# A two-block mixture-of-experts kernel: Sinkhorn's column sums as products with ones, and the first expert's gate applied one expert later

## The chip, the cores and the metric

The kernel runs on one core of a Trainium2 chip. The metric is the device time of one execution in microseconds (us); the median of three runs counts. A core has TensorE (PE in the profile, its weight loads PEld), VectorE (DVE), ScalarE (ACT), GpSimd (POOL) and SyncE (SP, which issues the DMAs). Each engine takes its own instructions strictly in program order, and waits on the others by semaphores.

## The reference, cut to what matters

The input passes through a thresholded attention, a first feed-forward block, and then the block that the change touches: eight experts, weighted by a gate that is balanced by eight Sinkhorn rounds.

```python
N, D = x.shape                      # 2304 tokens, 512 features
logits = x @ w_gate                 # E = 8 experts
P = np.exp(logits - logits.max())
for _ in range(8):
    P /= P.sum(1, keepdims=True) + 1e-09
    P /= P.sum(0, keepdims=True) + 1e-09
    P *= N / E
out = np.zeros((N, D), dtype=np.float32)
for e in range(E):
    h = np.maximum(x @ w1[e], 0.0)
    ye = h @ w2[e]
    out += P[:, e:e + 1] * ye
```

## The kernel before

After the attention, class `Moe` runs both feed-forward blocks as a list of units. Units 0 to 23 are the first block (kinds "a" and "b" in turn, three superblocks of 768 tokens); from unit 24 on there is one unit for each superblock, expert and quarter of the hidden features, in that order. Expert 0 of superblock 0 is units 24 to 27, expert 1 units 28 to 31, and so on. A unit's second products run during the next unit.

A unit has seven slots, and the order of all work is written out by hand in `run` (L775): in each slot `mm1` (L588) issues six first products into one of two PSUM banks, `px` or `py`; `pop` (L719) issues a share of the queued second products of the unit before (line L666, into `ye`; five in most slots, eight in slot 5); then one step of the generator `sinkhorn` (L748) is taken; then `evac` (L600) lets DVE and ACT read the bank: in slot 0 ACT copies `px` to `p1` (shown as `p`, L620), in slot 1 DVE makes `u` (L623), in slot 3 `v` (L626), in slots 4, 5 and 6 `c` (L640). In slots 2, 4, 5 and 6 ACT makes `hh`, the rounded Relu (L661), and one slot later DVE makes the rest `hl` (L662). Slots 0, 2 and 4 write `px`, the others `py`; slot 2 adds to what slot 0 left, slot 6 to what slot 5 left. So slot 4 may write `px` only when `hl` of slot 2 has read it, and slot 6 adds to `py` only when `c` of slot 5 has read it.

POOL prepares the next unit's weights in five pieces (`prep1`, L520): differences `wt` (L530, L533, L536) and the rests `w1l` (L537, L540, L542), with ACT's copies `w1h` between them. ACT's copy L539 waits for `wt` of L536, and L542 for that copy. DVE makes the rest `w2l` (L565) in slot 5.

The gate: `gate` (L733) computes the logits of a superblock; those of the last one are done in unit 25. `sinkhorn` starts there. It takes the maximum over all partitions (DVE L754, POOL `partition_all_reduce` L755), the exponential (ACT L758), and then eight rounds of two steps, one step a slot. The first step has the row sums, their reciprocals, the row scaling and the column sums on each partition (DVE, L761 to L765), and POOL's `partition_all_reduce` over the partitions (L766). The second step has four DVE operations (L768 to L771) that scale the columns. The rounds fill units 26, 27 and the first four slots of unit 28. `p`, the tile `prob` of 128 partitions x 18 chunks x 8 experts, is scaled in place.

`accumulate` (L708) takes the second products of a finished expert: expert 0 is copied to `acc` by ACT with the gate `p` as scale (L713), every later expert is multiplied by its gate and added by DVE (L715). For expert 0 of superblock 0 this falls in unit 28 and the first slots of unit 29.

Of the kernel before, what the change touches and what calls it, by code (L numbers as in the profile page):

```python
# [16 lines left out]
# the square of the float32 whose bits are a float64's high word at 2**-126  # L17
# [11 lines left out]
# when the x of the next superblock is split: (slots from the start of the last unit, slot that takes it)  # L29
SPLITS_AT = ((0, 0), (1, 1), (2, 2), (3, 3), (8, 4), (9, 5), (10, 6))  # L30
# pieces of conversion and products of W34 in each slot of two head pairs
# [20 lines left out]
def attention(k):  # L52
    """x^T (features on partitions) of all batches, with the W34 product as filler of the tensor engine."""
# [162 lines left out]
    def pv(j):  # L216
        """One product of a quarter's five: twenty a pair."""
# [102 lines left out]
class W34:  # L320
    """W34 = w3 @ w_out: float64 inputs to float32, then products, in pieces between the attention's."""
# [75 lines left out]
    def convert(self, s, more):  # L397
        """One more piece; it waits while the products still need the buffers."""
        self.slot = s
        self.owed += more  # L400
        if not self.owed or self.gen is None or self.held and self.nw3 - 3 >= self.mm // 12:
            return
        self.owed -= 1
        if next(self.gen, self) is self:
            self.gen = None
# [35 lines left out]
def to_f32(k, pool, raw, out):  # L441
    """Round float64 values, as pairs of 32-bit words, to float32; below float32's normal range gives zero."""
# [22 lines left out]
class Moe:  # L465
    """Both feed-forward blocks. First products by one level of Winograd's form of Strassen's algorithm:
    x (tokens x features) and the first weights are cut into 2 x 2 blocks, seven block products a unit."""

    # slot: (combination of x, combination of weights, bank, adds to the bank)
# [27 lines left out]
    def rest(self):  # L497
        """What the second products need, once there is room."""
# [21 lines left out]
    def prep1(self, u):  # L520
        """Pieces that make the seven combinations of a unit's first weights, in two exact parts."""
# [57 lines left out]
    def xsplit(self, s, slot):  # L579
        """The combination of x that the product of this slot takes, in two exact parts."""  # L580
# [19 lines left out]
    def evac(self, u, slot):  # L600
        """Combines the products; the later half of the work of the slot before comes first."""
# [106 lines left out]
    def accumulate(self, e, s, tc):  # L708
# [3 lines left out]
        if e == 0:  # L712
            nc.scalar.activation(acc, self.yb[tc], AF.Copy, scale=p)  # L713
        else:
            nc.vector.scalar_tensor_tensor(out=acc, in0=self.yb[tc], scalar=p, in1=acc, op0=ALU.mult, op1=ALU.add)  # L715
# [3 lines left out]
    def pop(self, slot):  # L719
        """One slot's share of the second products, more where the next slot's product waits for this one's."""  # L720
# [12 lines left out]
    def gate(self, s, slot):  # L733
        """A third of the logits of a superblock, in the bank that is free after this slot's product."""
# [13 lines left out]
    def sinkhorn(self):  # L748
        nc, p = self.nc, self.p
        small = self.pool.tile([128, 64], F32, name="small")  # L750
        m, g = small[:, 0:1], small[:, 1:2]
# [3 lines left out]
        nc.gpsimd.partition_all_reduce(g, m, 128, bass_isa.ReduceOp.max)  # L755
        yield
# [3 lines left out]
        for _ in range(8):  # L760
# [5 lines left out]
            nc.gpsimd.partition_all_reduce(gcol, col, 128, bass_isa.ReduceOp.add)  # L766
            yield
            nc.vector.tensor_scalar(out=gcol, in0=gcol, scalar1=1e-9, scalar2=None, op0=ALU.add)  # L768
            nc.vector.reciprocal(col, gcol)
            nc.vector.tensor_scalar(out=col, in0=col, scalar1=float(NTOK // E), scalar2=None, op0=ALU.mult)  # L770
            nc.vector.tensor_tensor(out=p, in0=p, in1=col.unsqueeze(1).to_broadcast([128, NCH, E]), op=ALU.mult)  # L771
# [126 lines left out]
```

## Time and profile before

| what | value |
|---|---|
| median of three runs | 2405.67 us (2404.77 to 2406.38) |
| span of the profiled execution | 2403.0 us |
| its own time | not recorded apart; the three runs lie 1.8 to 3.4 us above the span |
| PE busy | 2255.6 us, 94% of the span |
| DVE, ACT, POOL busy | 1344.7, 983.7, 1298.1 us |
| chain that ended last | PE 75%, DVE 13%, issue 8%, ACT 2%, POOL 1% |

The span runs from the first to the last instruction of the execution that the profiler took. Shares of the whole span mix stages: attention, first block and experts have different limits. The row of granted clock in the page's slices shows 9 (full) nearly everywhere; the lowest values, 7 and 6, stand in slices 15 and 16 of 40, where the Sinkhorn rounds run. An idle time in the profile stands with the instruction that ended it and the operation that released it; "issue" is time in which an engine waited for nothing that the profile shows. Instructions that switch the code of POOL (MODIFY_POOL_CONFIG, shown on its queue and as ISA in the order) take hundredths of a microsecond themselves.

### The profile page before, as it was taken

How to read it: one execution, taken by the hardware profiler on the slowest of the kernel's cores; microseconds unless marked ns; L12 is line 12 of the kernel's file. 1: busy time of each engine (PE TensorE's matmuls, PEld its weight loads, DVE VectorE, ACT ScalarE, POOL GpSimd, SP SyncE). 2: the span in 40 equal slices, each digit the busy share in tenths (PEclk: the TensorE clock that was granted, in tenths of full speed). 3: DMA queues.
4: the chain of work that ended last, by engine and by line, in shares of the span. 5: the costliest groups of instructions: out<-in, count | busy, mean ns of one | idle time of the engine just before them, and what ended most of it. 6: DMA issues, size and time to landing. Idle time of an engine off the chain costs nothing.

```text
span 2403.0 us, 30418 instructions
## 1 busy us (share of the span) xinstructions
PE 2255.6 (94%) x11408; PEld 1927.3 (80%) x11408; DVE 1344.7 (56%) x2385; ACT 983.7 (41%) x1709; POOL 1298.1 (54%) x1178
## 2 busy tenths in 40 slices
PE   5999999998989963999999999999999999999999
PEld 4566666587978853899999999999999899999998
DVE  8999999856464522444444463444444634444444
ACT  5777777633333410333333344333333443333332
POOL 5887777676666511544444554444445644444441
PEclk9999999999999976999999999999999999999999
DMA  5334344121111110122222122222221222222111
GB/s 155 95 104 121 112 119 120 56 87 53 53 53 69 47 35 18 53 70 71 71 71 71 59 91 71 70 71 71 71 68 56 96 71 71 71 71 71 58 66 53
DMA packets 52820, 177.63 MB, mean 74 GB/s; under 512 B 6592, under 2 KB 6592, under 8 KB 52672
## 3 DMA queue, kind: packets, MB, share of 16 engines
q1 hardware_dynamic: 52672, 175.68, 22.9%
q8 instruction: 90, 1.47, 0.3%
q14 instruction: 58, 0.48, 0.1%
HBM read 164.64 MB, written 11.01 MB: 73 GB/s over the span
## 4 chain that ended last, share of the span: by engine, by line
PE 75%; DVE 13%; issue 8%; ACT 2%; POOL 1%; SPq 0%; DMA 0%; POOLq 0%; ACTq 0%; DVEq 0%
PE ye L666 35%; PE py L596 19%; PE px L596 14%; PE pv L232 3%; DVE p L159 3%; DVE nmx L144 2%; PE s L139 1%; DVE qs L111 1%; PE t L195 1%; DVE c L651 1%; DVE cva L455 1%; DVE xl L585 1%; DVE cva L452 1%; PE w L423 1%; ACT e L153 1%
## 5 line engine op out<-in xcount | busy, mean ns | idle before, releaser
L542 POOL TENSOR_TENSOR w1l<-wt,w1h 128x1024 fp32r<-128x1024 f32 x120 | 290.8, 2423 | 324.2 <-ACT w1h L539 317.5
L666 PE MATMUL ye<-w2l,hh 128*128 128x512 f32 x1152 | 452.8, 393 | 3.3 <-DVE w2l L565 3.3
L666 PE MATMUL ye<-w2h,hl 128*128 128x512 f32 x1152 | 455.4, 395 | 0.0
L666 PE MATMUL ye<-w2h,hh 128*128 128x512 f32 x1152 | 453.7, 394 | 0.0
L661 ACT ACTIVATE hh<-c 128x384 fp32r<-128x384 f32 x288 | 151.4, 526 | 623.3 <-DVE c L640 623.3
L596 PE MATMUL py<-xh,w1h 128*128 128x384 f32 x960 | 326.7, 340 | 42.4 <-DVE c L640 32.8
L537 POOL TENSOR_TENSOR w1l<-raw,w1h 128x256 fp32r<-128x256 f32 x120 | 91.9, 766 | 493.7 <-ACT w1h L531 493.7
L596 PE MATMUL py<-xh,w1l 128*128 128x384 f32 x960 | 325.2, 339 | 0.3 <-POOL w1l L542 0.3
L596 PE MATMUL py<-xl,w1h 128*128 128x384 f32 x960 | 325.3, 339 | 0.0
L596 PE MATMUL px<-xh,w1h 128*128 128x384 f32 x720 | 244.5, 340 | 29.7 <-DVE hl L662 29.7
L666 PEld LDWEIGHTS ye<-w2l,hh 128*128 128x128 f32 x1152 | 217.6, 189 | 36.6 <-DVE w2l L565 3.7
L666 PEld LDWEIGHTS ye<-w2h,hl 128*128 128x128 f32 x1152 | 218.4, 190 | 32.8
L596 PE MATMUL px<-xh,w1l 128*128 128x384 f32 x720 | 244.0, 339 | 0.0
L596 PE MATMUL px<-xl,w1h 128*128 128x384 f32 x720 | 243.7, 338 | 0.0
L596 PEld LDWEIGHTS py<-xh,w1h 128*128 128x128 f32 x960 | 182.5, 190 | 68.9 <-DVE c L640 37.0
L666 PEld LDWEIGHTS ye<-w2h,hh 128*128 128x128 f32 x1152 | 218.1, 189 | 24.1
L596 PEld LDWEIGHTS py<-xl,w1h 128*128 128x128 f32 x960 | 182.6, 190 | 18.1
L623 DVE TENSOR_TENSOR u<-py,p 128x384 f32<-128x384 f32 x120 | 66.8, 557 | 214.6 <-PE py L596 212.4
L596 PEld LDWEIGHTS py<-xh,w1l 128*128 128x128 f32 x960 | 182.5, 190 | 0.6 <-POOL w1l L542 0.6
L530 POOL TENSOR_TENSOR wt<-raw 128x512 f32<-128x512 f32 x120 | 162.3, 1352 | 34.7 <-issue 21.0
L596 PEld LDWEIGHTS px<-xh,w1h 128*128 128x128 f32 x720 | 137.2, 191 | 45.3 <-DVE hl L662 31.3
L662 DVE SCALAR_TENSOR_TENSOR hl<-c,hh 128x384 fp32r<-128x384 f32 x288 | 166.2, 577 | 12.8 <-ACT hh L661 3.3
(127 smaller groups left out, 4448.5 us busy)
## 6 DMA issues: line engine op xcount, KB each, us to landing
raw<-in_e SPq DMA_DIRECT2D x192, 512.0 KB, 4.3
r<-in_qk SPq DMA_DIRECT2D x60, 288.0 KB, 6.6
wraw<-in_w SPq DMA_DIRECT2D x32, 512.0 KB, 4.5
raw<-w_a SPq DMA_DIRECT2D x12, 512.0 KB, 4.4
raw<-w_b SPq DMA_DIRECT2D x12, 512.0 KB, 3.2
raw<-w SPq DMA_DIRECT2D x12, 512.0 KB, 3.7
rv<-in_vv SPq DMA_DIRECT2D x16, 320.0 KB, 3.0
out<-acc SPq DMA_DIRECT2D x18, 256.0 KB, 2.0
```

The costliest lines, as they stand in the source:

```text
L111: nc.vector.scalar_tensor_tensor(out=dst, in0=rq[64:128, h, o:o + 288], scalar=0.125, in1=f32(dst), op0=ALU.mult, op1=ALU.subtract)
L144: nc.vector.tensor_reduce(out=nmx[:, s % 18:s % 18 + 1], in_=ps[:, :, 0:288], axis=AX.XY, op=ALU.max, negate=True)
L159: nc.vector.scalar_tensor_tensor(out=p, in0=ps[:, :, 0:288], scalar=thr[:, s % 18:s % 18 + 1], in1=e, op0=ALU.is_ge, op1=ALU.mult, accum_o ...
L232: nc.tensor.matmul(ps[0:64, 0:288], lhsT=l, rhs=r, start=i == 0, stop=i == 4)
L530: nc.gpsimd.tensor_tensor(out=t[:, 0:2], in0=raw[:, 1:3], in1=raw[:, 0:2], op=ALU.subtract)
L537: nc.gpsimd.tensor_tensor(out=wl[:, 0], in0=raw[:, 0], in1=f32(wh[:, 0]), op=ALU.subtract)
L542: nc.gpsimd.tensor_tensor(out=wl[:, 3:7], in0=t, in1=f32(wh[:, 3:7]), op=ALU.subtract)
L596: self.nc.tensor.matmul(out, lhsT=w[:, wi, o], rhs=x[xi][:, d], start=n == 0 and not adds, stop=n == 5, skip_group_check=True)
L623: tt(out=self.u2, in0=py, in1=self.p1, op=ALU.add)
L661: nc.scalar.activation(hi, src, AF.Relu)
L662: self.later.append(lambda: nc.vector.scalar_tensor_tensor(out=lo, in0=src, scalar=0.0, in1=f32(hi), op0=ALU.max, op1=ALU.subtract))
L666: self.queue.append((out.shape[-1], lambda: self.nc.tensor.matmul(out, lhsT=l, rhs=r, start=start, stop=stop, skip_group_check=True)))
```

## The change

Four things change. The column sums over the partitions are now one product of TensorE each: a tile `ones` (128 x 128, filled by POOL) as weights, the partial sums `col` as the 8 moving columns, into columns 384 to 391 of `px` or `py`, which the first products leave free. Adding 1e-9 reads PSUM, and the two multiplies that followed the reciprocal are one. The steps are placed anew: the maximum is issued at the end of unit 25, the exponential in slot 2 of unit 26, and the rounds begin in slot 3, with the product in the slot after the sums; products stand in slots 4 and 6 of unit 26, 1, 3 and 5 of unit 27, and 0, 2 and 4 of unit 28. And expert 0 of superblock 0 is copied without its gate; `acc` is multiplied by it when expert 1 is added, in unit 32. Besides, comments are gone, which moves line numbers.

```diff
@@ accumulate
-        if e == 0:
+        if e == 0 and s == 0:
+            nc.scalar.activation(acc, self.yb[tc], AF.Copy)
+        elif e == 0:
             nc.scalar.activation(acc, self.yb[tc], AF.Copy, scale=p)
         else:
+            if e == 1 and s == 0:
+                nc.vector.tensor_scalar(out=acc, in0=acc, scalar1=self.p[:, tc, 0:1], scalar2=None, op0=ALU.mult)
             nc.vector.scalar_tensor_tensor(out=acc, in0=self.yb[tc], scalar=p, in1=acc, op0=ALU.mult, op1=ALU.add)
@@ sinkhorn
+        ones = self.pool.tile([128, HT], F32, tag="c2", name="ones", bufs=2)[:, 0:128]
+        nc.gpsimd.memset(ones, 1.0)
...
         nc.gpsimd.partition_all_reduce(g, m, 128, bass_isa.ReduceOp.max)
+        yield
+        yield
         yield
...
             nc.vector.tensor_reduce(out=col, in_=p.rearrange("p c e -> p e c"), axis=AX.X, op=ALU.add)
-            nc.gpsimd.partition_all_reduce(gcol, col, 128, bass_isa.ReduceOp.add)
+            bank = yield
+            ps = bank[:, HT:HT + E]
+            nc.tensor.matmul(ps, lhsT=ones, rhs=col, start=True, stop=True, skip_group_check=True)
+            nc.vector.tensor_scalar(out=gcol, in0=ps, scalar1=1e-9, scalar2=None, op0=ALU.add)
+            nc.vector.reciprocal(col, gcol)
+            nc.vector.scalar_tensor_tensor(out=p, in0=p, scalar=float(NTOK // E),
+                                           in1=col.unsqueeze(1).to_broadcast([128, NCH, E]), op0=ALU.mult, op1=ALU.mult)
             yield
-            nc.vector.tensor_scalar(out=gcol, in0=gcol, scalar1=1e-9, scalar2=None, op0=ALU.add)
-            nc.vector.reciprocal(col, gcol)
-            nc.vector.tensor_scalar(out=col, in0=col, scalar1=float(NTOK // E), scalar2=None, op0=ALU.mult)
-            nc.vector.tensor_tensor(out=p, in0=p, in1=col.unsqueeze(1).to_broadcast([128, NCH, E]), op=ALU.mult)
-            yield
@@ run
-                next(sink, None)
+                if sink:
+                    try:
+                        sink.send(self.xy[1 if slot < 4 else 0])
+                    except StopIteration:
+                        sink = None
...
                         sink = self.sinkhorn()
+                        next(sink)
```

POOL from the start of Sinkhorn on, before (L755 and L766 are the reductions, an ISA row alone is a switch of POOL's code, L530 to L540 prepare the weights of units 27 and 28):

```order
L755 ISA
L755 ISA small<-small 128x1 [waits DVE_49]
L530 ISA
L530 TENSOR_TENSOR wt_7940<-raw_27_7772 128x512 [waits DMAHW0_49,Pool_49]
L533 TENSOR_TENSOR wt_7940<-raw_27_7772,wt_7940 128x256 [waits Pool_49]
L766 ISA
L766 ISA small<-small 128x8 [waits DVE_49]
L536 ISA
L536 TENSOR_TENSOR wt_7940<-raw_27_7772,wt_7940 128x256 [waits Pool_49]
L537 TENSOR_TENSOR w1l_7939<-raw_27_7772,w1h_7938 128x256 [waits PE_49,Activation_49]
L540 TENSOR_TENSOR w1l_7939<-raw_27_7772,w1h_7938 128x512 [waits Activation_49]
L766 ISA
```

The same place in the change, where L757 fills `ones` and L762 is the one reduction left:

```order
L757 MEMSET ones 128x128 [waits DVE_49]
L762 ISA
L762 ISA small<-small 128x1 [waits DVE_49]
L530 ISA
L530 TENSOR_TENSOR wt_7942<-raw_27_7772 128x512 [waits DMAHW0_49,Pool_49]
L533 TENSOR_TENSOR wt_7942<-raw_27_7772,wt_7942 128x256 [waits Pool_49]
L536 TENSOR_TENSOR wt_7942<-raw_27_7772,wt_7942 128x256 [waits Pool_49]
L537 TENSOR_TENSOR w1l_7941<-raw_27_7772,w1h_7940 128x256 [waits PE_49,Activation_49]
L540 TENSOR_TENSOR w1l_7941<-raw_27_7772,w1h_7940 128x512 [waits Activation_49]
L542 TENSOR_TENSOR w1l_7941<-wt_7942,w1h_7940 128x1024 [waits Activation_49]
L530 TENSOR_TENSOR wt_8087<-raw_28_7925 128x512 [waits DMAHW2_49,Pool_49]
```

The reductions between the weight pieces are gone, and with them all switches but one there and one back.

DVE in slots 3 and 4 of unit 27, before, from the row scaling on (`small` holds the sums and their reciprocals):

```order
L764 TENSOR_TENSOR prob<-prob,small 128x144 [waits DVE_49]
L765 TENSOR_REDUCE small<-prob 128x8 [waits DVE_49]
L662 SCALAR_TENSOR_TENSOR hl_8070<-px,hh_8069 128x384 [waits Activation_49]
L626 TENSOR_TENSOR v_3_8152<-py,u_27_1_8112 128x384 [waits PE_49]
L768 TENSOR_SCALAR small<-small 128x8 [waits Pool_49]
L769 RECIPROCAL small<-small 128x8 [waits DVE_49]
L770 TENSOR_SCALAR small<-small 128x8 [waits DVE_49]
L771 TENSOR_TENSOR prob<-prob,small 128x144 [waits DVE_49]
L640 TENSOR_TENSOR c_4_8172<-px,v_3_8152 128x384 [waits PE_49]
```

The same place in the change, from the row scaling of slot 2 to the first row of slot 4's block:

```order
L773 TENSOR_TENSOR prob<-prob,small 128x144 [waits DVE_49]
L774 TENSOR_REDUCE small<-prob 128x8 [waits DVE_49]
L778 TENSOR_SCALAR small<-py 128x8 [waits PE_49]
L779 RECIPROCAL small<-small 128x8 [waits DVE_49]
L780 SCALAR_TENSOR_TENSOR prob<-prob,small 128x144 [waits DVE_49]
L662 SCALAR_TENSOR_TENSOR hl_8064<-px,hh_8063 128x384 [waits Activation_49]
L626 TENSOR_TENSOR v_3_8144<-py,u_27_1_8105 128x384
L770 TENSOR_REDUCE small<-prob 128x18 [waits DVE_49]
```

The three operations behind the product (L778 to L780) now stand ahead of `hl` and `v` in slot 3; before, the sums stood there and the wait for POOL came in slot 4, ahead of `c`.

PE at the end of slot 3 of unit 27, before:

```order
L666 MATMUL ye_5146<-w2h_8000,hl_7919 128x512
L666 MATMUL ye_5147<-w2h_8000,hh_7918 128x512
L666 MATMUL ye_5147<-w2l_8044,hh_7918 128x512
L596 MATMUL px<-xh_4956,w1h_7938 128x384 [waits DVE_49]
L596 MATMUL px<-xl_4963,w1h_7938 128x384
L596 MATMUL px<-xh_4956,w1l_7939 128x384
```

And in the change:

```order
L666 MATMUL ye_5146<-w2h_7997,hh_7923 128x512
L666 MATMUL ye_5146<-w2l_8040,hh_7923 128x512
L666 MATMUL ye_5146<-w2h_7997,hl_7924 128x512
L666 MATMUL ye_5147<-w2h_7997,hh_7923 128x512
L666 MATMUL ye_5147<-w2l_8040,hh_7923 128x512
L777 MATMUL py<-small,ones 128x8 [waits DVE_49]
L596 MATMUL px<-xh_4956,w1h_7940 128x384 [waits DVE_49]
```

The product of `ones` and `small` stands behind the slot's five second products and ahead of the next slot's first product, which waits for DVE in both.

## Rows read from the trace of the kernel before

**Rows 1.** Windows: us, busy time of PE, PEld, DVE, ACT, POOL, then granted clock, DMA.

```profile
992.00:2380.00 1388.00, 1388.00 (x6965) 1252.49 (x6964) 636.63 (x1026) 487.49 (x828) 663.70 (x539) 1.00 0.21 70
845.69:991.41 145.72, 81.65 (x314) 70.52 (x312) 43.32 (x112) 24.35 (x43) 35.80 (x36) 0.73 0.08 25
```

**Rows 2.** Timelines of PE and ACT: start us, us, instruction, idle time before it.

```profile
845.69 0.34 PE L596 MATMUL px<-xh,w1h 128*128 128x384 f32 x1
...
846.73 0.39 PE L666 MATMUL ye<-w2h,hh 128*128 128x512 f32 x1
...
991.41 0.34 PE L596 MATMUL px<-xh,w1h 128*128 128x384 f32 x1
...
992.71 0.49 ACT L620 ACTIVATE p<-px 128x384 f32<-128x384 f32 x1 [0.90 <-PE px L596]
...
1008.25 0.49 ACT L620 ACTIVATE p<-px 128x384 f32<-128x384 f32 x1 [0.90 <-PE px L596]
```

**Rows 3.** Waits of the stretch 838 to 975 us: total, times, longest.

```profile
DVE small L768 <- POOL small L766: 79.6, 8, 12.6
...
PE px L596 <- DVE hl L662: 29.7, 3, 11.4
...
PE py L596 <- DVE c L640: 25.5, 3, 8.8
...
PE py L596 <- DVE u L623: 5.2, 1, 5.2
```

**Rows 4.** Timeline of POOL around the second reduction.

```profile
853.09 1.28 POOL L530 TENSOR_TENSOR wt<-raw 128x512 f32<-128x512 f32 x1 [7.18 <-issue]
854.45 0.72 POOL L533 TENSOR_TENSOR wt<-raw,wt 128x256 f32<-128x256 f32 x1
861.16 0.43 POOL L766 PARTITION_ALL_REDUCE small<-small  x1 [5.99 <-issue]
```

**Rows 5.** Timeline of PE: the end of its first idle time in unit 26.

```profile
863.10 0.69 PE L596 MATMUL px<-xh,w1h 128*128 128x384 f32 x1 [8.50 <-DVE hl L662]
```

**Rows 6.** Timeline of PE: the gate products of one slot.

```profile
842.99 1.85 PE L740 MATMUL px<-wg,x 128*128 128x8 f32 x16
```

**Rows 7.** Timeline of DVE: behind the second column sum, and the third row sum.

```profile
877.46 0.17 DVE L768 TENSOR_SCALAR small<-small 128x8 f32<-128x8 f32 x1 [11.48 <-POOL small L766]
...
878.33 0.55 DVE L640 TENSOR_TENSOR c<-py,v 128x384 f32<-128x384 f32 x1
878.80 0.55 DVE L662 SCALAR_TENSOR_TENSOR hl<-c,hh 128x384 fp32r<-128x384 f32 x1
...
880.40 0.30 DVE L761 TENSOR_REDUCE small<-prob 128x18 f32<-128x144 f32 x1
...
881.92 0.55 DVE L640 TENSOR_TENSOR c<-py,u 128x384 f32<-128x384 f32 x1
```

**Rows 8.** Timelines of POOL and DVE: subtractions that overlap, and one in unit 30.

```profile
970.39 2.38 POOL L542 TENSOR_TENSOR w1l<-wt,w1h 128x1024 fp32r<-128x1024 f32 x1
...
970.95 2.24 DVE L662 SCALAR_TENSOR_TENSOR hl<-c,hh 128x384 fp32r<-128x384 f32 x1 [3.31 <-ACT hh L661]
...
998.54 2.40 POOL L542 TENSOR_TENSOR w1l<-wt,w1h 128x1024 fp32r<-128x1024 f32 x1 [2.97 <-ACT w1h L539]
```

**Rows 9.** PE waits and windows with granted clock in two earlier stretches.

```profile
667.00 0.39 PE L666 MATMUL ye<-hl,w2h 128*128 128x256 f32 x1 [1.50 <-DVE hl L653]
...
803.61 0.45 PE L596 MATMUL py<-xh,w1h 128*128 128x384 f32 x1 [2.24 <-DVE c L640]
...
664.00:672.00 8.00, 5.50 (x35) 5.30 (x36) 5.26 (x9) 3.69 (x7) 4.84 (x5) 1.00 0.36 136
808.00:812.00 4.00, 2.98 (x12) 2.98 (x13) 2.55 (x4) 2.93 (x6) 1.28 (x2) 0.66 0.72 259
```

**Rows 10.** Groups by line and shape: two DVE operations of 512 elements.

```profile
L715 DVE SCALAR_TENSOR_TENSOR acc<-ye,prob,acc 128x512 f32<-128x512 f32 x126 | 91.9, 744 | 3.8 <-PE ye L666 3.8
...
L460 DVE TENSOR_SCALAR cvs<-cvq 128x512 int32<-128x512 int32 x40 | 17.6, 441 | 0.3
```

More of the change, by code (lines that the diff above doesn't have):

```diff
@@ L788, in run @@
             pass
-        sink = iter(())
+        sink = None
         gates = {8 * s + (12 if s + 1 < NSB else 9): s for s in range(NSB)}
@@ L809, in run @@
                 self.pop(slot)
-                next(sink, None)
+                if sink:
+                    try:
+                        sink.send(self.xy[1 if slot < 4 else 0])
+                    except StopIteration:
+                        sink = None
                 self.evac(u, slot)
```

## The prediction

> **What bounds the kernel now.** I read the windows first, then the waits of the stretch in which the Sinkhorn work runs, then the timelines of POOL, DVE and PE there. From 992 to 2380 us TensorE is busy 1388.00 of 1388.00 us at granted clock 1.00; in 845.69 to 991.41, four units of the first expert (units 26 to 29), it is busy 81.65 of 145.72 us at a mean clock of 0.73 [rows 1]. An edit there is worth what TensorE's idle and slow time in it is worth. How long should four units take? The same copy `p<-px` of slot 0 comes at 992.71 and at 1008.25, so an undisturbed unit is 15.54 us, one of its seven slots 2.2 us, and four units are 62.2 us. Unit 26 starts at 845.69, unit 30 at 991.41 [rows 2]. So the hole costs 145.72 - 62.16 = **83.5 us**, its clock loss included. The change can't win more here.
>
> Who ends the waits? DVE's first operation behind each reduction (L768) waits for POOL 8 times, 79.6 us in all; PE in turn waits 29.7 us for `hl`, 25.5 us for `c` and 5.2 us for `u`, all of them DVE operations that stand behind L768 in DVE's queue [rows 3]. On POOL a PARTITION_ALL_REDUCE takes 0.43 us, but it stands 5.99 us behind the operation before it, and the operation after a reduction stands 7.18 us behind that, with nothing waited for ("issue") [rows 4]: a round is 13.6 us of POOL, while its two slots of TensorE are 4.4 us.
>
> **What the change removes.** Eight reductions on POOL with those gaps (the order shows only TENSOR_TENSORs behind the first reduction), and DVE's wait for them. The first expert's ACT copies no longer need `p`. If nothing took their place, the gain would be 83.5 us.
>
> The Trainium skill speaks against the change: GPSIMD Engine Reference, section Engine selection, gives a reduction along partitions to GpSimd. Its section Instruction dispatch prices the first call of a freshly loaded kernel at about 6 us, which the 5.99 us of [rows 4] bears out; of a second gap behind the call it says nothing, and by that price alone the change would free 8 x 6 = 48 us of POOL's time (an estimate from that page), not 8 x 13.6 = 109.
>
> **What stays.** One reduction (the maximum, L755), whose result is now read in slot 2 of unit 26 instead of slot 0. The gap behind it still holds POOL until 853.09 [rows 4]. The weights of unit 27 then take 2 x 1.28 + 3 x 0.72 + 2.38 = 7.1 us [rows 4, 8] and end near 860.3; unit 27 starts at 845.69 + 15.54 = 861.2 and wants the last piece one slot later. So that gap is covered, with 3 us; without the cover unit 27 would wait. In the trace too TensorE ran through it: its first idle time in the stretch ends at 863.10 and is DVE's [rows 5]. Cost 0. The fill of `ones` stands ahead of that reduction in POOL's idle time: 0.
>
> **What is added on TensorE.** Eight products of 8 columns. Nearest row: 8 gate products (16 instructions) take 1.85 us [rows 6], 0.23 us each, so 1.85 us. Bounds: half of it if much lies beside other work, double if one product alone isn't pipelined, 0.9 to 3.7 us. I take 1.85.
>
> **What is added on DVE's way.** In a product slot DVE now waits for the product, does three small operations, and only then the slot's own work. Four such operations took from 877.46 to 878.33, 0.87 us; without the extra multiply 0.65. The column-sum block (five operations) takes from 880.40 to 881.92, 1.52 us [rows 7]. Six first products of a slot take 846.73 - 845.69 = 1.04 us, so five second ones take 1.15; ACT's copy comes 1.30 us after the slot's start, 0.26 us after the sixth [rows 2]. The new product's answer I put at 0.3 us after TensorE is through with its slot. From then on TensorE waits wherever the next slot's product needs what DVE does behind the block. The order tells where (slots 0 to 6):
> 1. Unit 26, slot 5 to 6: slot 6 adds to `py` after `c` of slot 5. DVE has from slot 4's product on 0.3 + 0.65 + 0.47 (`c`) + 1.52 + 0.55 (`c`) + 0.06 = 3.55 us to do; TensorE has slot 5, with eight second products 2.9 us: **0.7 us**.
> 2. Unit 27, slot 3 to 4: `px` is rewritten after `hl` has read it, and `hl` stands behind the three operations: 0.3 + 0.65 + 0.55 [rows 7] + 0.06 = **1.55 us**.
> 3. Unit 27, slot 5 to 6: the same with `c`: **1.55 us**.
> 4. Unit 28, slot 3 to 4: from slot 2's product on 0.3 + 0.65 + 1.52 + 0.55 + 0.06 = 3.1 us against slot 3's 2.2: **0.9 us**.
> The other four products (unit 26 slot 6, unit 27 slot 1, unit 28 slots 0 and 4) delay results that have a slot or more to spare: 0. Sum 4.7 us.
>
> **Collisions of DVE and POOL.** While POOL's `w1l` subtraction ran from 970.39 for 2.38 us, a DVE `hl` that began at 970.95 took 2.24 us instead of 0.55 [rows 7, 8]; it ended 0.4 us after POOL did. Both its inputs, `c` and `hh`, lie in SBUF. The row and the column scaling of `p` have two such inputs too; no row shows them beside POOL, which stood still then. Bounds: 0, or the 2.4 us of the POOL operation each time they meet. I take that they are held as `hl` was. Where do they meet? POOL is late in unit 26, so its last subtraction runs about 857.9 to 860.3; the block of slot 5 reaches its row scaling at about 858.9: held some 1.5 us, on stall 1. In unit 30 the subtraction starts 7.1 us into the unit (998.54) [rows 2, 8]; in unit 28 ACT has two `acc` copies ahead of the weight copy that it waits for, so about 8.4 us; the row scaling of slot 3 comes 6.6 + 0.25 + 0.3 + 0.65 + 0.84 = 8.6 us in: held up to 2.2 us, on stall 4. A few tenths decide whether they meet; I take 2. On stalls 2 and 3 a few tenths. Together **3.9 us**.
>
> The Trainium skill, GPSIMD Engine Reference, section Key points, says that GpSimd shares its SBUF interfaces with VectorE and contends with operations of two SBUF inputs. By it the 3.9 us belong in the sum; by the undisturbed scalings of p alone the sum would be 3.9 us smaller.
>
> **Clock.** After a wait of 2.24 us and others close behind it TensorE fell to the lower of its two levels (1.2 GHz): the mean of 808 to 812 is 0.66. After waits of up to 1.50 us it stayed at 1.00 (664 to 672) [rows 9]. Stalls 1 and 4, with the collisions 2.2 and 2.9 us, are as long as the first of these. I take one such spell, 4 x (1 - 0.66) = **1.4 us**; bounds 0 and four, 5.6 us.
>
> **The first expert's gate.** In unit 32 six DVE multiplies of 128x512: 0.44 us (nearest in kind: 512 elements, one tensor input) to 0.74 us (nearest in shape) [rows 10], 2.6 to 4.5 us in all, behind the slots' own DVE work. Their cover is DVE's idle half, 636.63 busy of 1388 us [rows 1]. Three fall together at the unit's end and put off `u` of the next unit by up to 1.5 us; slot 3 wants it, 4.4 - 1.04 - 0.26 - 0.55 = 2.5 us after it is normally done. Cost 0; at most 1 us, if they meet POOL too.
>
> **Sum.** 83.5 - 1.85 - 4.7 - 3.9 - 1.4 = 71.6 us. The span is 2403.0 us; the three times lie 1.8 to 3.4 us above it, and that part stays. 2403.0 - 71.6 = 2331.4, with the median's 2.67 us beside it **2334.0 us**.
>
> **The rivals.**
> A, the forecast: 2334, own range 2329 to 2339 (products 0.9 to 3.7, spells 0 to 2, collisions 1 to 5).
> B, no collision and no spell: 2405.67 - 83.5 + 1.85 + 4.7 = 2328.7. For it: undisturbed scalings within the 1.52 us block; against: `hl` of 2.24 us.
> C, collisions on all four stalls (another 1.5 us on each of 2 and 3) and a spell after each (3 x 1.4): 2334.0 + 7.2 = 2341. For it: a wait of 2.24 us began a spell; against: waits of 1.50 us did not.
> D, the gap behind a reduction isn't the reduction's, POOL keeps it, and only 8 x 5.99 us go: 2405.67 - 47.9 + 11.9 = 2370. Against it: behind another POOL operation the next starts at once (854.45 behind 853.09) [rows 4].
> The price on the Trainium skill's page, GPSIMD Engine Reference, Instruction dispatch, would make it D.
> E, **slower**: each round's product now stands in TensorE's own in-order queue; if the way from product over DVE's scalings and sums to the next product is longer than two slots, TensorE waits in every round. It decides from 71.6 / 8 = 9.0 us a round on. With 13.6 us, a wait as long as POOL's round, it is 2334 + 109 = 2443. Against: the way is 0.3 + 0.65 + 1.52 us plus DVE's own work, under 4.4, and the longest hold in the rows is 2.4.
> F, the change doesn't do what it says: TensorE's idle time came from something that stays, about 2405. Against: 60.4 us of it end on DVE operations queued behind L768 [rows 3].
>
> **How the numbers follow.** A 0.66, B 0.13, C 0.14, D 0.03, E 0.02, F 0.02. The likeliest is A, 2334.0. The range 2326 to 2342 holds A, nearly all of B and more than half of C, some 0.85. Faster by over 0.2% (4.8 us, about what a measurement of this kernel can tell from no change) are A to D, 0.96; within it F, 0.02; slower E, 0.02.
>
> **What would show it.** In the changed profile: one PARTITION_ALL_REDUCE, and no "issue" gaps on POOL after 853; unit 26 to unit 30 in about 74 us; waits of PE at exactly those four places, ended by `c`, `hl`, `c` and `hl`, the first and the last 2 to 3 us; a scaling of `p` of over 1 us beside a `w1l`; one or two spells of low clock; no change from unit 30 on. Wrong would be: PE waiting for the new product's own input, a wait for `w1l` in unit 27, or for `u` in unit 33.

## The result, and the profile after

The changed kernel takes **2337.83 us** (median; 2337.07 to 2341.5) where the kernel before takes 2405.22 (2403.77 to 2406.38): ratio 0.9722, 95% interval 0.9708 to 0.9736, 67.4 us less. The forecast was 2334.0, with 2326 to 2342 as its range.

Where did the time go? Cut both spans where unit 26 and unit 30 start. Windows (us, busy time of PE, PEld, DVE, ACT, POOL, granted clock, DMA), of the kernel before:

```profile
0.00:845.69 845.69, 766.29 (x4040) 587.43 (x4041) 654.51 (x1232) 468.47 (x833) 598.57 (x604) 0.98 0.30 89
991.41:2403.00 1411.59, 1407.66 (x7057) 1269.30 (x7055) 646.87 (x1042) 490.91 (x834) 663.70 (x539) 1.00 0.21 70
```

and of the changed kernel, the three parts and a piece of the last:

```profile
0.00:849.02 849.02, 769.41 (x4040) 591.05 (x4041) 653.99 (x1232) 468.56 (x833) 598.63 (x605) 0.98 0.30 89
849.02:925.12 76.10, 67.21 (x329) 59.48 (x328) 46.21 (x105) 23.92 (x43) 31.81 (x28) 0.98 0.14 48
925.12:2336.70 1411.58, 1407.63 (x7057) 1269.30 (x7055) 651.43 (x1048) 490.88 (x834) 664.05 (x539) 1.00 0.20 70
...
925.00:2315.00 1390.00, 1390.00 (x6976) 1254.36 (x6975) 641.78 (x1033) 488.51 (x831) 664.05 (x539) 1.00 0.20 70
```

The last part is the same to 0.01 us (1411.59, 1411.58), and from 925 to 2315 TensorE is busy all the time, the gate's six multiplies in unit 32 included. Four units of the first expert take **76.10 us** instead of the 145.72 of [rows 1]: 69.6 less, to a floor of 62.2. The first part, which the change hardly touches (the maximum and the fill of `ones` stand at its end), took 3.3 us longer in this execution. 69.6 - 3.3 = 66.3 is the difference of the spans (2403.0, 2336.7); the profiled execution's own time was 2338.47.

TensorE's waits of the stretch, from its timeline (start us, us, instruction, idle time before it):

```profile
866.02 0.44 PE L596 MATMUL py<-xh,w1h 128*128 128x384 f32 x1 [3.05 <-DVE c L640]
868.73 0.41 PE L596 MATMUL px<-xh,w1h 128*128 128x384 f32 x1 [0.35 <-DVE small L778]
...
873.64 0.39 PE L777 MATMUL py<-small,ones 128*128 128x8 f32 x2 [0.28 <-DVE small L774]
879.93 0.44 PE L596 MATMUL px<-xh,w1h 128*128 128x384 f32 x1 [1.30 <-DVE hl L662]
886.48 0.44 PE L596 MATMUL py<-xh,w1h 128*128 128x384 f32 x1 [1.31 <-DVE c L640]
891.31 0.45 PE L596 MATMUL py<-xh,w1h 128*128 128x384 f32 x1 [0.30 <-DVE small L778]
896.34 0.45 PE L596 MATMUL py<-xh,w1h 128*128 128x384 f32 x1 [0.26 <-DVE small L778]
900.84 0.45 PE L596 MATMUL px<-xh,w1h 128*128 128x384 f32 x1 [2.04 <-DVE hl L662]
```

Four long ones, at the four places of the forecast, each ended by the operation forecast there: 3.05, 1.30, 1.31 and 2.04 us, in place of waits such as the 8.50 us of [rows 5]. Four short ones of 0.26 to 0.35 us were not forecast: three wait for DVE's addition (L778) to read the product with ones out of the bank whose other columns the next first product writes, and one is the product with ones waiting for its own input, the partial sums (L774).

POOL's timeline, the reduction that is left and three operations behind it:

```profile
848.86 0.57 POOL L762 PARTITION_ALL_REDUCE small<-small  x1 [9.67 <-DVE small L761]
856.25 1.28 POOL L530 TENSOR_TENSOR wt<-raw 128x512 f32<-128x512 f32 x1 [6.83 <-issue]
...
861.09 2.46 POOL L542 TENSOR_TENSOR w1l<-wt,w1h 128x1024 fp32r<-128x1024 f32 x1
...
897.33 2.38 POOL L542 TENSOR_TENSOR w1l<-wt,w1h 128x1024 fp32r<-128x1024 f32 x1 [3.94 <-ACT w1h L539]
```

One PARTITION_ALL_REDUCE, 6.83 us of "issue" behind it (7.18 in [rows 4]), and no such gap later.

DVE's timeline, the column scaling (L780), the adding of 1e-9 (L771) and the row scaling (L773), beside POOL's weight work and undisturbed, with the row sum (L770) and the reciprocal (L772) between them:

```profile
860.49 0.81 DVE L780 SCALAR_TENSOR_TENSOR prob<-prob,small 128x144 f32<-128x144 f32 x1
...
861.69 0.28 DVE L770 TENSOR_REDUCE small<-prob 128x18 f32<-128x144 f32 x1
862.01 1.57 DVE L771 TENSOR_SCALAR small<-small 128x18 f32<-128x18 f32 x1
863.62 0.27 DVE L772 RECIPROCAL small<-small 128x18 f32<-128x18 f32 x1
863.92 1.13 DVE L773 TENSOR_TENSOR prob<-prob,small 128x144 f32<-128x144 f32 x1
...
874.51 0.31 DVE L780 SCALAR_TENSOR_TENSOR prob<-prob,small 128x144 f32<-128x144 f32 x1
...
875.53 0.18 DVE L771 TENSOR_SCALAR small<-small 128x18 f32<-128x18 f32 x1
...
876.04 0.31 DVE L773 TENSOR_TENSOR prob<-prob,small 128x144 f32<-128x144 f32 x1
...
897.75 2.14 DVE L773 TENSOR_TENSOR prob<-prob,small 128x144 f32<-128x144 f32 x1
```

Either scaling takes 0.31 us alone. Begun 0.42 us into a subtraction of 2.38 us the row scaling takes 2.14, much as `hl` did in [rows 8] (2.24). And L771, which has one tensor input, takes 1.57 instead of 0.18. Ahead of TensorE's first long wait the excess is (0.81 - 0.31) + (1.57 - 0.18) + (1.13 - 0.31) = 2.71 us, ahead of the fourth 2.14 - 0.31 = 1.83.

### The profile page after: what moved, and what is told of

Its sections match the earlier page's. It is cut to its first block, busy times and chain, and to the rows that moved or that the text cites. A ratio compares the mean times of both kernels' runs of the same rounds, so it can differ in the third digit from the quotient of the medians.

```text
span 2336.7 us, 30411 instructions
## 1 busy us (share of the span) xinstructions
PE 2244.3 (96%) x11424; PEld 1919.8 (82%) x11424; DVE 1351.6 (58%) x2383; ACT 983.4 (42%) x1709; POOL 1294.5 (55%) x1171
## 3 DMA queue, kind: packets, MB, share of 16 engines
q8 instruction: 90, 1.47, 0.3%
## 4 chain that ended last, share of the span: by engine, by line
PE 79%; DVE 14%; issue 3%; ACT 2%; DMA 0%; SPq 0%; ACTq 0%; DVEq 0%
PE ye L666 37%; PE py L596 20%; PE px L596 15%; DVE p L159 3%; PE pv L232 3%; DVE nmx L144 2%; DVE qs L111 1%; PE s L139 1%; DVE c L651 1%; PE t L195 1%; DVE cva L455 1%; PE w L423 1%; DVE cva L452 1%; DVE xl L585 1%; ACT e L153 1%
## 5 line engine op out<-in xcount | busy, mean ns | idle before, releaser
L530 POOL TENSOR_TENSOR wt<-raw 128x512 f32<-128x512 f32 x120 | 162.3, 1353 | 20.7 <-issue 6.8
L661 ACT ACTIVATE hh<-px 128x384 fp32r<-128x384 f32 x96 | 47.4, 494 | 276.2 <-PE px L596 276.2
```

Of the source, the lines that this page charges most:

```text
L530: nc.gpsimd.tensor_tensor(out=t[:, 0:2], in0=raw[:, 1:3], in1=raw[:, 0:2], op=ALU.subtract)
L661: nc.scalar.activation(hi, src, AF.Relu)
```

## The experiments

The theory: the gain is the reductions' gaps off POOL; what is left between 76.1 and 62.2 us is waits at the four places, lengthened by DVE and POOL meeting, and a spell of low clock. Rivals: the gap is not the reduction's own (D), the late gate has a part in it, or the rest belongs to the rounds wherever they stand.

| run | time, beside before on the same chip (us) | ratio (95%) | four units (us) |
|---|---|---|---|
| the change | 2337.83, 2405.22 | 0.9722 (0.9708 to 0.9736) | 76.10 |
| e1 no rounds | 2325.22, 2407.41 | 0.9661 (0.9647 to 0.9675) | 63.49 |
| e2 a copy for each round's reduction | 2338.21, 2407.41 | 0.9714 (0.9699 to 0.9728) | 76.33 |
| e3 late gate alone | 2407.29, 2407.41 | 0.9999 (0.9990 to 1.0009) | 146.42 |
| e4 no weight work | 2330.55, 2407.41 | 0.9683 (0.9669 to 0.9697) | 69.34 |
| e5 evacuation first in slots 3, 5 | 2333.65, 2406.27 | 0.9690 (0.9672 to 0.9707) | 72.97 |
| e6 evacuation first in all slots | 2334.34, 2406.27 | 0.9695 (0.9677 to 0.9713) | 74.21 |
| e7 rounds spread | 2329.18, 2406.38 | 0.9684 (0.9670 to 0.9697) | 68.74 |
| e8 the same, w2h first | 2330.35, 2406.38 | 0.9687 (0.9674 to 0.9700) | 67.73 |
| e9 the change again | 2337.11, 2406.38 | 0.9714 (0.9701 to 0.9728) | 77.16 |
| e10 steps merged | 2333.34, 2407.72 | 0.9694 (0.9681 to 0.9707) | 68.17 |

The times are medians; the last column is read from one profiled execution each (that of e5 took 2340.63 us).

**e2: is the gap the reduction's own?** In the kernel before, POOL copies each column sum instead of reducing it, so the sum over the partitions is left out; every wait between DVE and POOL stays.

```diff
-            nc.gpsimd.partition_all_reduce(gcol, col, 128, bass_isa.ReduceOp.add)
+            nc.gpsimd.tensor_scalar(out=gcol, in0=col, scalar1=1.0, scalar2=None, op0=ALU.mult)
```

> The kernel before, with each round's POOL reduction replaced by a POOL copy of the partial sums (left out: the sum over partitions). Theory, the gaps around the reduction are its own and are what TensorE paid for: POOL's issue gaps go, units 26 to 29 take 66 to 76 us, time 2326 to 2338 us. Rival D of the prediction, the gap behind a reduction isn't the reduction's: about 2370 us. Second rival, the hop DVE to POOL to DVE is the cost whatever POOL does: over 2390 us.

76.33 us for the four units and 0.9714: the change's own numbers, without its products or its gate. That they agree so closely is chance: e2 has other waits of TensorE (3.70, 0.89, 1.16 and 2.64 us) and a mean clock of 0.93 instead of 0.98. POOL's timeline:

```profile
854.95 0.73 POOL L533 TENSOR_TENSOR wt<-raw,wt 128x256 f32<-128x256 f32 x1
855.66 0.28 POOL L766 TENSOR_SCALAR small<-small 128x8 f32<-128x8 f32 x1
855.92 0.72 POOL L536 TENSOR_TENSOR wt<-raw,wt 128x256 f32<-128x256 f32 x1
...
861.26 0.23 POOL L766 TENSOR_SCALAR small<-small 128x8 f32<-128x8 f32 x1 [2.71 <-DVE small L765]
861.46 2.37 POOL L542 TENSOR_TENSOR w1l<-wt,w1h 128x1024 fp32r<-128x1024 f32 x1
```

The copy stands between weight operations with no gap on either side. So both gaps of [rows 4] go with the reduction, and D falls. That each round still goes to POOL and back makes DVE wait 4.5 us in all, in three places (79.6 us in [rows 3]).

But the gaps don't come with every reduction. Once in the kernel before, two of them stand one behind the other, with no weight operation between (POOL's timeline):

```profile
939.41 0.43 POOL L766 PARTITION_ALL_REDUCE small<-small  x1 [5.75 <-issue]
944.07 0.40 POOL L766 PARTITION_ALL_REDUCE small<-small  x1 [4.23 <-DVE small L765]
951.57 1.25 POOL L530 TENSOR_TENSOR wt<-raw 128x512 f32<-128x512 f32 x1 [7.10 <-issue]
```

The second begins 0.1 us after DVE's sum is there (943.97), and DVE waits 0.53 us for it. So POOL stands still where it changes from weight operations to a reduction or back, seven times each way in the eight rounds, and not because of the reduction alone. Whether it would have been enough to keep the weight operations out from between the reductions was not tried.

**e3: the late gate alone**, on the kernel before.

```diff
-        if e == 0:
+        if e == 0 and s == 0:
+            nc.scalar.activation(acc, self.yb[tc], AF.Copy)
+        elif e == 0:
...
+            if e == 1 and s == 0:
+                nc.vector.tensor_scalar(out=acc, in0=acc, scalar1=self.p[:, tc, 0:1], scalar2=None, op0=ALU.mult)
```

> The kernel before with the second part of the change alone: expert 0 copied unscaled, its gate applied with expert 1. Theory, it is a matter of freedom for the placing and gives little by itself, since DVE and POOL hold TensorE up anyway: 2402 to 2406 us. Rival, ACT's wait of 13.2 us for the gate held up TensorE (the wait of 3.3 us for w2l at 975 and the low clock behind it): 2395 to 2400 us. The six multiplies: no wait of TensorE in units 32 and 33; if they cost, up to 1 us more.

No difference: 0.9999, within a tenth of a per cent either way, and PE's first wait is 8.50 us as in [rows 5]. The wait for `w2l` that the rival meant stays too (3.54 us, 3.33 before). In the kernel before a copy on ACT did wait for the last scaling of `p` (its timeline):

```profile
961.23 0.69 ACT L713 ACTIVATE acc<-ye,prob 128x512 f32<-128x512 f32 x1 [13.21 <-DVE prob L771]
```

In e3 none does, and nothing comes of it: DVE and TensorE are late anyhow. In the profile after, the copies begin at 895.23, 9.5 us ahead of the last scaling (904.78), so there the late gate lets the rounds end later. What it is worth in that place was not tried.

**e1: no rounds at all**, the floor of this program.

```diff
-        for _ in range(8):
+        for _ in range(0):
```

> The changed kernel without its eight Sinkhorn rounds (left out: both normalisations; the maximum and the exponential stay). Theory, the hole of 83.5 us is the rounds' alone and the one reduction left is covered: units 26 to 29 take 62 to 63 us, the time is 2405 - 83.5 = about 2322 us (2320 to 2325). Rival, part of the hole or of the 15.6 us between 2337.8 and 2322 belongs to something that stays (the first reduction, the late gate, the front of the program): 2326 or more, with TensorE waits left in units 26 to 29.

63.49 us, 1.33 above the floor of 62.16 and a little over the expected 62 to 63. One wait is left, in unit 27 (PE's timeline, and ACT's in the unit before):

```profile
867.53 0.50 PE L666 MATMUL ye<-w2l,hh 128*128 128x512 f32 x1 [1.02 <-DVE w2l L565]
...
860.53 1.06 ACT L539 ACTIVATE w1h<-wt 128x1024 fp32r<-128x1024 f32 x1 [4.90 <-POOL wt L536]
861.49 1.04 ACT L560 ACTIVATE w2h<-raw 128x1024 fp32r<-128x1024 f32 x1
```

The gap behind the one reduction makes `wt` late, so ACT's copy `w1h` (L539) waits 4.90 us; `w2h` and `hh` stand behind it. DVE's `hl` then comes late and runs beside POOL's last subtraction (2.26 us instead of 0.55), and `w2l` behind it takes 2.32 instead of 1.22. I had looked for `w1l` alone and said "covered": it costs 1.0 us where no other wait hides it. The wait of 1.02 us costs 1.33, some 0.3 more than the idle time that the profile gives it.

**e4: without POOL's and ACT's weight work.** Units 27 to 29 take the first weights of unit 26; the preparation of theirs is left out. Everything else is the changed kernel.

```diff
+        if u in (27, 28, 29):
+            self.w1[u] = self.w1[26]
+            return
```

> The changed kernel with units 27 to 29 taking unit 26's first weights (left out: POOL's and ACT's preparation of three units' weights, so POOL stands still beside the rounds). Theory, DVE's operations on p were held by POOL's subtractions: L771 and L773 take 0.18 and 0.31 us in all rounds, the wait for c in unit 26 falls from 3.05 to about 0.6 us, the wait for hl in unit 28 from 2.04 to about 0.8, no low clock behind it; time 2337.8 less 3.5 to 5.5, 2332 to 2334.5 us. Rival, the waits come from the place in DVE's queue alone: they stay, 2336 to 2339 us.

69.34 us against 76.10, at granted clock 1.00. The window:

```profile
849.78:919.12 69.34, 65.35 (x330) 58.19 (x328) 38.77 (x105) 18.41 (x34) 10.38 (x10) 1.00 0.16 54
```

The block that held up stall 1 (DVE's timeline; lines are 3 higher here):

```profile
862.27 0.18 DVE L774 TENSOR_SCALAR small<-small 128x18 f32<-128x18 f32 x1
862.48 0.27 DVE L775 RECIPROCAL small<-small 128x18 f32<-128x18 f32 x1
862.78 0.31 DVE L776 TENSOR_TENSOR prob<-prob,small 128x144 f32<-128x144 f32 x1
```

0.18 and 0.31 us again. Stalls 2 and 3 stay at 1.31, stalls 1 and 4 shrink to 0.34 and 0.24: by 3.05 - 0.34 = 2.71 and 2.04 - 0.24 = 1.80 us, to a few hundredths the excess that DVE's rows gave (2.71 and 1.83). They shrink further than expected (0.6 and 0.8), and the time, 2330.55, lies below the expected 2332 to 2334.5. So collisions (4.5 us) and the spell (1.7, below) make up 6.2 of the 6.8 us between the two kernels.

**e5 and e6: the evacuation ahead of the Sinkhorn step**, in slots 3 and 5 or in all: the operation that TensorE needs no longer stands behind the step.

```diff
+                ahead_of = slot in (3, 5)    # e6: True
+                if ahead_of:
+                    self.evac(u, slot)
...
-                self.evac(u, slot)
+                if not ahead_of:
+                    self.evac(u, slot)
```

> The changed kernel with DVE's own work of the slot ahead of the Sinkhorn step in slots 3 and 5 (hl and v, c and hl first). Theory, the four long TensorE waits come from the place of the Sinkhorn step in DVE's queue: all four go (3.05, 1.30, 1.31, 2.04 us and what the restarts add, some 8.3 us, and the spell of low clock, 1.7 us), units 26 to 29 take 65 to 67 us, time 2326.5 to 2330 us. Rival, the rounds' own chain (product, scaling, sums, product) is too long for two slots: TensorE waits for the column sums at the products instead, 2333 to 2338 us.

> As the run with slots 3 and 5, but the slot's own work first in every slot. Theory: in the other slots nothing waits for it, so within 0.2% of that run, 2326 to 2330 us; the short waits of TensorE for the read of the product's bank (0.26 to 0.35 us) may grow since that read moves back. Rival: the read moves behind hl, which waits for ACT, and the product's bank comes free later: waits of 1 us and more in front of slot 0 of unit 27 and slots 1 and 3 of unit 28, 2330 to 2334 us.

The waits for `c` and `hl` go in e5, but the step now stands behind, and its products come late (PE's timeline of e5):

```profile
872.18 0.39 PE L777 MATMUL px<-small,ones 128*128 128x8 f32 x2 [2.00 <-DVE small L774]
873.62 0.66 PE L596 MATMUL px<-xh,w1h 128*128 128x384 f32 x1 [1.05 <-DVE small L778]
```

and behind them a spell of low clock (window):

```profile
876.00:880.00 4.00, 4.00 (x13) 3.46 (x13) 1.09 (x4) 1.28 (x3) 1.96 (x2) 0.53 0.41 167
```

The theory is right on the waits that go, the rival on the time: 2333.65 lies in its range, since much of what the order wins turns into waits for L774 and L778 (5.2 us in all). What the order is worth is not sharp: the four units are 3 to 4 us shorter than in the change's two profiles, the ratio is 0.9690 against 0.9714 and 0.9722, and its interval touches that of e9. In e6 such waits (1.68 us) and waits for `hh` and `c` (1.98, 1.47) eat a little more; the two times differ by less than their intervals.

**e7 and e8: the rounds spread out.** Steps only in slots 0, 1, 2 and 6, from unit 27 on, two rounds a unit, all products in the bank of `py`. e8 also puts ACT's `w2h` ahead of `w1h` in unit 26, which e1 asked for. e9 is the changed kernel again, beside them.

```diff
         nc.scalar.activation(p, p, AF.Exp, bias=g, scale=1.0)
         yield
+        yield
...
-                if sink:
+                if sink and slot in (0, 1, 2, 6):
                     try:
-                        sink.send(self.xy[1 if slot < 4 else 0])
+                        sink.send(self.xy[1])
...
+                if u == 26 and slot == 3:    # e8; its later place is skipped
+                    self.prep2(u, 0)
```

> The changed kernel with its Sinkhorn steps taken only in slots 0, 1, 2 and 6 of a unit, from slot 0 of unit 27 on: a block of sums in slot 0 or 2, the product with ones in slot 1 or 6, two rounds a unit, all products in the bank of py, the last two in unit 30. Nothing is left out. Theory (what the rounds still cost in the changed kernel is their place: behind a product that TensorE needs at once, and beside POOL's weight work): the four waits of 1.3 to 3.1 us and the spell of low clock go; four units take 62.2 + 1.2 (the wait for w2l seen without rounds) + 6 x 0.23 + at most 1 = 65 to 66 us against 76.1, and the time is 8 to 11 us below that of the changed kernel, 2326 to 2330 beside a kernel before of 2405.7. Rival (the ten or so us of loss belong to the rounds wherever they stand: other waits take their place, in units 29 and 30): four units plus the first slots of unit 30 lose as much, the time is within 4 us of the changed kernel's, 2334 or more.

> The same as the one with the spread rounds, and in slot 3 of unit 26 ACT makes the copy w2h of the second weights ahead of the copy w1h of the next first weights. Theory (the one reduction that is left holds POOL up, which puts off ACT's w1h, behind it w2h, and so w2l, for which TensorE waited 1.02 us in unit 27): that wait goes, four units take about 1.2 us less than with the spread rounds alone, 64 to 65 us. Rival (the wait for w2l is POOL's or DVE's own lateness and not ACT's order): it stays, or is replaced by a wait for w1l at the start of unit 27, and four units take as long or longer.

> The changed kernel itself, on the same chip as the two with spread rounds, so that the three can be compared directly: 0.972 of the time before, about 2338 us, four units about 76 us with the waits of 3.1, 1.3, 1.3 and 2.0 us.

e7 is 7.9 us faster than e9 on the same chip, and its interval lies below the other's: **a version that beats both kernels**. Its four units take 68.74 us (77.16 in e9), not the 65 to 66 of the theory, and unit 30 has 1.5 us more in it. In e8 the wait for `w2l` is gone (0.62 in e7) and the four units are 1.0 us shorter, near the expected 1.2; in the times that is too small to see. What is left in e7 (PE's and DVE's timelines; lines are 1 higher here):

```profile
884.76 0.39 PE L778 MATMUL py<-small,ones 128*128 128x8 f32 x2 [0.76 <-DVE small L775]
...
907.37 0.44 PE L596 MATMUL px<-xh,w1h 128*128 128x384 f32 x1 [1.67 <-DVE hl L662]
...
882.18 0.70 DVE L772 TENSOR_SCALAR small<-small 128x18 f32<-128x18 f32 x1
...
903.95 2.46 DVE L774 TENSOR_TENSOR prob<-prob,small 128x144 f32<-128x144 f32 x1
```

In unit 28 the block of slot 0 meets POOL's first subtractions (L772 takes 0.70 us, the row scaling L774 1.04), so the product of slot 1 waits 0.76 us (1.10 in unit 27); and in unit 29 the scaling (L774) takes 2.46 us beside the last one, so `hl` is late. The same two mechanisms, at other places and smaller.

**e10: product and next block in one step**, in slots 1 and 6, out of POOL's way, on top of e8.

```diff
-        yield        # one of three ahead of the exponential
...
-                if sink and slot in (0, 1, 2, 6):
+                if sink and slot in (1, 6):
...
-            yield        # the one behind the column scaling
```

> The version with spread rounds and w2h first, with the product's three operations and the next block of sums taken together, in slots 1 and 6 of a unit only (first block in slot 1 of unit 27, first product in slot 6 of unit 27, last one in slot 1 of unit 31). Nothing is left out. With steps in slots 0, 1, 2 and 6 the trace showed what was left: the block of slot 0 took 2.85 us instead of 1.52 beside POOL's first w1l subtractions (0.7 us ahead of the product of slot 1, in units 27 and 28), and a row scaling held for 2.46 us beside POOL's last one (1.67 us before slot 4 of unit 29). Theory (these are collisions with POOL and a product one slot behind its sums): a block that begins right behind slot 6 and one behind slot 1 meet POOL's idle times, each sum has two slots or more to its product, and the waits of 0.76 to 1.67 us go: the four units take 64 to 65 us against 67.7, and the time is 2 to 4 us below that of the spread version. Rival (whatever DVE does in a burst of 2.4 us puts off an operation that TensorE needs): new waits on hl or c of 1 us or more take their place, and the time is the same or up to 3 us longer.

The theory's gain does not come, and the rival is nearer: 0.9694 against e8's 0.9687, 68.17 us against 67.73. The collisions are nearly gone in units 28, 30 and 31, but a burst of eight operations stands ahead of `u` or `c` in all of units 28 to 31 (DVE's and PE's timelines):

```profile
884.17 0.17 DVE L777 TENSOR_SCALAR small<-py 128x8 f32<-128x8 f32 x1 [1.52 <-PE py L776]
...
886.52 0.55 DVE L623 TENSOR_TENSOR u<-py,p 128x384 f32<-128x384 f32 x1
...
887.13 0.44 PE L596 MATMUL py<-xh,w1h 128*128 128x384 f32 x1 [0.71 <-DVE u L623]
...
905.88 0.44 PE L596 MATMUL py<-xh,w1h 128*128 128x384 f32 x1 [1.55 <-DVE u L623]
```

From 884.17 to 886.52 DVE works only for the step, and TensorE waits 0.71 us for the `u` behind it. In unit 29 it waits 1.55 us, and there 0.9 us are still collisions (the column scaling takes 0.58 instead of 0.31, the adding of 1e-9 0.82 instead of 0.18).

## Why the prediction was right, and where a size was off

- **What bounds it, the hole of 83.5 us, the gaps on POOL: right**, and shown by e2 and e3. Only the 13.6 us of POOL are not the price of every round: of two reductions in a row the second had no gap ahead of it. The Trainium skill's price (GPSIMD Engine Reference, Instruction dispatch: about 6 us of loading at the first call of a freshly loaded kernel) has its gap ahead of the call; the gap behind it, 6.83 us in the profile after, was no smaller, and e2 shows that it goes when the reductions go. By that page's price alone the time would have been D's 2370.
- **The products: right.** One that nothing holds up starts at 859.73 in the profile after; the next slot's first two products start at 859.87 and 860.13, so 0.40 us pass instead of 0.17. That is 0.23 us each, 1.85 in all.
- **The four stalls without collision: right in place, too long by 0.2 to 0.7 us.** Forecast 0.7, 1.55, 1.55 and 0.9; e4 shows 0.34, 1.31, 1.31 and 0.24, 3.2 us of idle time instead of 4.7. On stalls 2 and 3 the sum held the product twice: from its start (878.35 in the profile after) to the next first product (879.93) are 1.58 us, but 0.28 of them are the product itself.
- **The collisions: on the two stalls foreseen, and mis-sized.** Stall 1 has 2.7 us of them instead of 1.5, since the forecast held only the operations with two tensor inputs and L771 was held for 1.4 us besides, to the end of the subtraction that it met (863.55); the row scaling (1.13 us) was then held by POOL's next operation, L530 from 863.62, which the forecast had not counted. Stall 4 has 1.8 instead of 2. Together 4.5 instead of 3.9. That L771 can be held follows from two sections of the Trainium skill read together, of which I used half: GPSIMD Engine Reference, Key points, names operations with two SBUF inputs and also those in a two-port mode, and VectorE: DVE Perf Modes, Mode 2×_2P, says that an operation with one tensor in SBUF and a constant can use both read ports. The trace agrees as far as it goes: L771 is held (1.57 us), the row sum beside the same subtraction (0.28) is not, and neither is the reciprocal (0.27) beside the operation that POOL does next. Which mode ran, no row shows.
- **Missing from the sum:** the four short waits of 0.26 to 0.35 us, 1.2 us in all. One of them, the product waiting 0.28 us for its own input, is among the signs that the prediction called wrong; it came once in eight products, and E would need it in every round, and long.
- **The clock: one spell, as taken**, behind the fourth wait. Windows of the profile after, and of e9 behind its first wait (3.36 us):

```profile
866.00:870.00 4.00, 3.63 (x19) 3.39 (x20) 3.57 (x7) 0.86 (x2) 0.50 (x1) 1.00 0.18 44
901.50:905.00 3.50, 3.50 (x13) 3.12 (x12) 0.59 (x3) 0.00 (x0) 1.10 (x2) 0.54 0.00 0
```

```profile
865.00:870.00 5.00, 4.26 (x16) 3.82 (x17) 3.79 (x8) 0.71 (x2) 0.79 (x2) 0.67 0.24 67
```

  It cost 3.5 x (1 - 0.54) + 2 x (1 - 0.95) = 1.7 us (the second term from 905 to 907), forecast 1.4. That there was one is in part luck: which wait starts a spell is not settled: after 3.05 us the clock stayed at 1.00, after 2.04 it fell to about half (1.2 of 2.4 GHz); in e9, the same kernel, the first wait brought it down, and behind the fourth (2.05 us) it was 1.00 (902 to 910). The prediction read in [rows 9] that waits of up to 1.50 us leave the clock alone; that does not hold. Behind a wait of 1.50 us in the first block, with the same short waits ahead of it in both (0.65, 0.65 and 0.9 us), the profiles before and after have:

```profile
504.00:508.00 4.00, 3.88 (x26) 3.88 (x27) 2.12 (x5) 2.51 (x6) 2.00 (x2) 1.00 0.52 204
506.00:510.00 4.00, 3.93 (x16) 3.93 (x17) 2.16 (x5) 1.72 (x4) 1.97 (x2) 0.59 0.47 184
```

- **The first reduction "covered, cost 0": wrong by a wait of 1.0 us** (e1), hidden here behind other waits. **The gate's multiplies, cost 0: right**, TensorE busy 1390.00 of 1390.00 us.

So the four units: 76.10 - 62.16 = 13.9 us lost, 11.9 forecast. Measured: waits 7.7, short waits 1.2, products 1.85, spell 1.7, together 12.4; the remaining 1.5 is what the eight waits cost beyond their idle time, 0.2 each (0.3 in e1). The fourth long one shows how: the matmul ahead of it counts as busy for 0.39 us, where another would have started after 0.23, and behind it the second first product starts 0.28 us after the first (900.84, 901.12) instead of 0.17. That the sum of the losses came within 2 us owes something to errors that cancel: the stalls were 1.5 us too long, while collisions (0.6), spell (0.3), short waits (1.2) and this rest (1.5) were too small or missing. Rivals B, D, E and F are out. The time lies between A's 2334 and C's 2341, and the trace decides for A: collisions on two stalls, though on more operations, and one spell.

**The rest of the miss is not the change's.** The forecast of the gain was 71.6, the stretch gave 69.6, the medians 67.4. Unit 26 starts at 845.69 in the profile before and at 849.02 after, but also at 849.73 in e3, at 849.52 in e1, at 846.63 in e2, at 845.67 in e7 and at 854.25 in e5, though up to there e3 is the kernel before and e1, e5 and e7 are the changed kernel. The first part moves by several us from execution to execution. Of the 3.3 us between the two profiles, 2.0 have come by the first unit's copy `p<-px` (484.42, 486.44), and 1.4 come with the spell behind the wait of 1.50 us: a unit of 10.79 us takes 12.22, TensorE busy all the time. Later differences cancel. Why the spells come and go, and what moves the first 485 us, is open.

## What to carry to other kernels

Ask not how long an instruction runs but how long its engine does nothing before and behind it: 0.43 us of reduction between weight operations was 13.6 us of POOL, and a small operation in its place, on POOL (e2) or on TensorE, won the same 67 to 69 us. When a chain moves from a slow engine into the queues of busy ones, what remains is order: what TensorE needs next stands behind it, or beside a neighbour's memory traffic. Count the latter for operations with one tensor input too, and spread a chain that has time (e7, another 8 us) in pieces short enough that nothing urgent waits behind one (e10).

## What the runs showed of the hardware that I had not expected

- Behind a PARTITION_ALL_REDUCE the next elementwise POOL operation starts 6.6 to 7.7 us later, with nothing waited for, also when it is the only reduction left (6.83 after, 6.73 in e2, 7.27 in e7). A second reduction directly behind the first started 0.1 us after its input (944.07 before).
- DVE's addition of a constant to 128x18 numbers takes 1.57 us instead of 0.18 beside a POOL subtraction, while a reduction over a free axis beside it keeps its 0.28. POOL's own subtractions beside these held operations, 2.46 and 2.38 us, are as long as those of [rows 8], 2.38 and 2.40. But POOL is held too: in e8 its L530, begun 2.4 us into DVE's `w2l`, took 2.16 us instead of 1.28 (`w2l` itself 3.42 instead of 1.22).
- Waits of 3.05 and 3.36 us at the same place of the same kernel left the clock at 1.00 in one execution and brought it to 0.67 in the mean of 5 us in another; a wait of 1.50 us, with the same waits ahead of it, was followed by 1.00 in one and by 0.59 over 4 us in another.
